# Global keys behind 96 own keys of each block, and one normalising step for a block on VectorE

## The chip, the core and the metric

The kernel runs on one core of one Trainium2 chip. The metric is the device time of one execution in microseconds (us); less is better. The engines of the core are named as in the profile: PE is TensorE (PEld its weight loads), DVE is VectorE, ACT is ScalarE, POOL is GpSimd, SP is SyncE, whose queue issues the DMAs.

## The reference: local and global attention, then a gated FFN

There are 8 batches of 8 heads, 512 local and 32 global tokens, heads of 64 dimensions, all in float32. Global tokens attend to all 544 keys. A local token attends to the 32 global keys and to local keys at most 32 positions away. The heads of a batch are then joined to rows of 512, and every row goes through a gated feed-forward network (FFN) with 1536 hidden units.

```python
k_all = np.concatenate([k_g, k_l], axis=2)
out_g = np.matmul(sm(scale * np.matmul(q_g, k_all.transpose(0, 1, 3, 2))), v_all)
mask = np.abs(pos[:, None] - pos[None, :]) <= 32
s_ll = np.where(mask, scale * np.matmul(q_l, k_l.transpose(0, 1, 3, 2)), -1e9)
s_lg = scale * np.matmul(q_l, k_g.transpose(0, 1, 3, 2))
out_l = np.matmul(sm(np.concatenate([s_lg, s_ll], axis=-1)), np.concatenate([v_g, v_l], axis=2))
x = concat([out_g, out_l], axis=2), heads joined: (8 * 544, 512)
out = (sigmoid(x @ w_gate) * (x @ w_val)) @ w_out
```

`sm` is a softmax with the row's maximum subtracted and 1e-9 added to the sum.

## The kernel before, in words

**Tiles of the attention.** A head's 512 local queries are four blocks of 128. The host lays the keys out so that the keys of a block stand in one window of 224 columns (`WIN`): 32 own keys left of the block, 64 of the block's first keys, the 32 global keys, the block's other 64 keys, and 32 own keys right of it. Neighbouring windows overlap and start 160 columns apart (`BLK`). Block 0 has no left and block 3 no right part, so their windows are 192 wide (`span`). `local_unit` works on two blocks at once: (0, 1) or (2, 3) where a chunk has two blocks, and (0, 3), called the joint unit, and then (1, 2), where it has four. It has four stages, between which other work is emitted:

1. scores into PSUM (L234); then VectorE adds the mask and finds the maximum (L248), and ScalarE takes the exponential with its sum (L251), both into `s_sb`, which has one buffer;
2. the reciprocal of the sums (L254, L255), and the normalised probabilities into `p_buf` (`scaled`, L214 to L219). Per block there is one instruction for the main columns (2 x 64, the block's own keys) and one for the side columns (2 or 3 pieces of 32: left, global, right). Which engine does it goes by the table `NORM`: VectorE (L218) for converted heads and the first chunk, and ScalarE (L216) or VectorE in turn for the second chunk and the first four heads of the third;
3. transposes of `p_buf` in tiles of 128 columns on PE (L271; 4, or 3 in the joint unit), copied out of PSUM by ScalarE (L282, or L279 for native heads), the remainder by VectorE (L283);
4. the products with V on PE (L302 and L303, or L294 and L295), two for each block: the main tile `VM[j]` and the side tile `VS[j]` of V, which the host filled in the same order, with zero rows where a transposed tile holds columns that aren't the block's.

**Two number formats.** From the fifth head of the third chunk on, heads are *converted*: every operand is split into a rounded part and a remainder (`split_qk` with L197 to L200, `split_v` with L210 and L211), and a product is made from the parts; there are 52 of these heads. The first 20 heads are *native* and use float32 matmuls. Of these, 12 take part in global scores within the same chunks (the eight of the second chunk and four of the third).

**Global rows.** For each head `global_scores` makes the 32 x 544 scores of the global queries in three steps: two of 256 columns (a 64-column half of all four windows, L319) and one of 32 columns (L321), each once for a native and twice for a converted head. ScalarE copies them into `pg` (L323, L324), and for four heads together `global_group` normalises, transposes five tiles (L341) and multiplies with V (L356 or L362).

**FFN and weights.** `ffn_stream` runs over chunks of up to 512 rows and 12 hidden tiles each: gate and value matmuls (L401), ScalarE's tanh, absolute value and exponential (L409 to L416) and VectorE's minimum (L414), VectorE's products (L421 to L425) with ScalarE's cast (L424), then the output matmuls (L438). The first two chunks have 256 rows and alternate. Each weight piece is loaded into one of three staging buffers and converted in `convert` by ScalarE (L137, L141), VectorE (L139, L140) and POOL (L142); the output weights go to DRAM and come back as `wo` (L429). `x_split` (L373, L374) brings the attention's result into the FFN's format.

**Order of the work.** Attention, splits, loads and conversions are events with due times in a list `queue`. `ffn_stream` yields after every few matmuls, a clock `now` advances by that amount, and all events that are due are emitted. Engines work through their own instructions in the emitted order, apart from places where `issue_after` or the scheduler moves an instruction, and wait for each other where data or buffers ask for it.

## Time and profile before

| what | value |
|---|---|
| median of 3 runs | 1164.27 us (1164.24 to 1165.34) |
| profiled execution | 1168.26 us, of which the span of the profile 1166.3 us |
| mean granted clock of PE | 0.997 |
| PE busy, of the span | 1148.5 us (98%) |
| VectorE busy | 747.2 us (64%), 2132 instructions |
| ScalarE busy | 751.9 us (64%), 1737 instructions |
| POOL busy | 413.9 us (35%) |

Busy time is the time in which at least one instruction of the engine was running by the profile. Matmuls are pipelined: a row gives the length of one from its start to its modelled end, and the distance between the starts of neighbours is what one costs in a stream. A wait is idle time of an engine in front of an instruction, with the engine or transfer that ended it. The granted clock is TensorE's, as a share of full speed.

### The profile page before, as it was taken

Reading aid. Unit: us, or ns where it says so; the run is one execution under the profiler, and the core shown is the slowest. Engines: PE = TensorE matmul, PEld = TensorE weight load, DVE = VectorE, ACT = ScalarE, POOL = GpSimd, SP = SyncE. Lnnn points to the kernel's source line nnn. Section 1 sums busy time; section 2 is a strip of 40 time slices with the busy share of each in tenths; the row PEclk is TensorE's granted clock in tenths of the full one; section 3 lists DMA queues with packets and bytes.
Section 4 is the critical chain, followed back from the end, with each engine's and each line's share of the span. In section 5 each row is a group of like instructions: output and inputs, shape, how many; then the busy total and the mean of one; then the engine's idle time right before and its main releaser. Section 6 shows DMA issues by size and latency. Waiting matters only on the chain.

```text
span 1166.3 us, 19141 instructions
## 1 busy us (share of the span) xinstructions
PE 1148.5 (98%) x6596; PEld 962.8 (83%) x6596; DVE 747.2 (64%) x2132; ACT 751.9 (64%) x1737; POOL 413.9 (35%) x408
## 2 busy tenths in 40 slices
PE   8999999999999999999999999999999999999998
PEld 6777788988888888888888888888888888888897
DVE  5667746666776677667676677667676677533343
ACT  5898867666676766667675676676675676432343
POOL 2434434424443444434443444334452443100000
PEclk9999999999999999999999999999999999999999
DMA  8888844334333333343443343343344342122143
GB/s 295 285 278 272 270 126 117 117 114 113 111 101 129 117 107 109 107 130 100 117 117 104 116 117 99 108 136 101 109 118 126 97 125 74 56 89 72 55 157 115
DMA packets 59489, 151.81 MB, mean 130 GB/s; under 512 B 6144, under 2 KB 19456, under 8 KB 59392
## 3 DMA queue, kind: packets, MB, share of 16 engines
q1 hardware_dynamic: 59392, 150.59, 42.4%
q8 instruction: 52, 0.85, 0.3%
q14 instruction: 45, 0.37, 0.1%
HBM read 135.36 MB, written 15.20 MB: 129 GB/s over the span
## 4 chain that ended last, share of the span: by engine, by line
PE 90%; ACT 3%; DMA 2%; DVE 2%; POOL 1%; issue 1%; SPq 0%; DVEq 0%; ACTq 0%; POOLq 0%
PE bank_g L401 23%; PE bank_o L438 23%; PE bank_v L401 23%; PE bank_x L234 5%; PE bank_y L271 4%; PE bank_x L319 2%; PE bank_x L302 2%; PE bank_x L303 2%; PE bank_x L362 1%; PE bank_o L110 1%; PE bank_x L294 1%; DMA wo<-wo_dram 1%; PE bank_y L341 1%; PE bank_x L295 1%; DMA xt<-in_w_val_dram 1%
## 5 line engine op out<-in xcount | busy, mean ns | idle before, releaser
L438 PE MATMUL bank_o<-wo,hh 128*128 128x512 f32 x1224 | 330.4, 401 | 3.3 <-ACT hh L424 1.7
L401 PE MATMUL bank_g<-xt,wg 128*128 128x512 f32 (+1 forms) x1440 | 330.8, 365 | 0.1
L401 PE MATMUL bank_v<-xt,wv 128*128 128x512 f32 (+1 forms) x1440 | 328.4, 364 | 0.0
L401 PEld LDWEIGHTS bank_g<-xt,wg 128*128 128x128 f32 x1440 | 237.1, 189 | 37.6 <-issue 2.7
L401 PEld LDWEIGHTS bank_v<-xt,wv 128*128 128x128 f32 x1440 | 237.2, 189 | 36.0 <-DVE t L306 1.5
L438 PEld LDWEIGHTS bank_o<-wo,hh 128*128 128x128 f32 x1224 | 218.0, 189 | 44.1 <-ACT hh L424 3.5
L251 ACT ACTIVATE s_sb<-s_sb,nm 128x192 f32<-128x192 f32 (+1 forms) x240 | 110.5, 462 | 96.0 <-DVE nm L248 95.6
L211 POOL TENSOR_TENSOR vhl<-v_raw,vhl 128x512 fp32r<-128x512 f32 x52 | 67.4, 1296 | 185.5 <-ACT vhl L210 102.7
L307 POOL TENSOR_TENSOR x<-t 64x256 f32<-64x256 f32 x104 | 76.6, 736 | 156.9 <-DVE t L306 130.9
L218 DVE TENSOR_SCALAR p_buf<-s_sb,r 128x128 f32<-128x128 f32 (+2 forms) x443 | 124.8, 312 | 6.3 <-PE bank_y L271 1.8
L198 POOL TENSOR_TENSOR kl<-qk_raw,qk_hi 128x704 fp32r<-128x704 f32 x52 | 88.7, 1705 | 111.8 <-ACT qk_hi L197 111.3
L424 ACT CAST hh<-bank_v 128x512 fp32r<-128x512 f32 (+1 forms) x120 | 62.7, 522 | 91.3 <-DVE bank_v L422 90.3
L409 ACT ACTIVATE th<-bank_g 128x512 f32<-128x512 f32 (+1 forms) x120 | 63.9, 532 | 86.6 <-PE bank_g L401 86.2
L414 DVE TENSOR_SCALAR mn<-bank_g 128x512 f32<-128x512 f32 (+1 forms) x108 | 67.5, 625 | 72.5 <-ACT th L409 72.5
L306 DVE TENSOR_TENSOR t<-bank_x,t 64x512 f32<-64x512 f32 x104 | 70.7, 680 | 66.8 <-ACT t L305 66.2
L248 DVE CUSTOM_DVE_ANT_0 s_sb<-bank_x,masks 128x192 f32<-128x192 f32 (+1 forms) x240 | 79.9, 370 | 38.7 <-PE bank_x L234 34.4
L421 DVE TENSOR_TENSOR bank_v<-bank_v,mn 128x512 f32<-128x512 f32 (+1 forms) x120 | 73.8, 615 | 48.1 <-PE bank_v L401 43.7
L425 DVE TENSOR_TENSOR hh<-bank_v,hh 128x512 fp32r<-128x512 f32 (+1 forms) x120 | 72.9, 608 | 32.6 <-ACT hh L424 30.6
L200 POOL TENSOR_TENSOR qk_hi<-qk_raw,qk_hi 64x256 fp32r<-64x256 f32 x104 | 80.2, 792 | 4.1
L283 DVE TENSOR_TENSOR pt<-bank_y,pt 128x384 fp32r<-128x384 f32 x104 | 64.2, 618 | 21.5 <-ACT pt L282 21.3
L422 DVE SCALAR_TENSOR_TENSOR bank_v<-th,bank_v 128x512 f32<-128x512 f32 (+1 forms) x120 | 73.3, 611 | 1.7
L271 PE MATMUL bank_y<-ident,p_buf 128*128 128x128 f32 x440 | 70.0, 275 | 1.9 <-DVE mn L414 0.9
(108 smaller groups left out, 1654.0 us busy)
## 6 DMA issues: line engine op xcount, KB each, us to landing
wo<-wo_dram SPq DMA_DIRECT2D x116, 512.0 KB, 3.4
qk_raw<-in_qk_dram SPq DMA_DIRECT2D x104, 312.0 KB, 4.5
v_raw<-in_v_dram SPq DMA_DIRECT2D x52, 256.0 KB, 2.6
out_dram<-ob SPq DMA_DIRECT2D x34, 256.0 KB, 2.9
xt<-in_w_gate_dram SPq DMA_DIRECT2D x12, 512.0 KB, 5.1
xt<-in_w_val_dram SPq DMA_DIRECT2D x12, 512.0 KB, 4.8
xt<-in_w_out_dram SPq DMA_DIRECT2D x12, 512.0 KB, 5.6
v_nat<-in_v_dram SPq DMA_DIRECT2D x8, 512.0 KB, 8.0
```

The costliest lines, as they stand in the source:

```text
L198: nc.gpsimd.tensor_tensor(kl, t[:, K0:Q1], hi[:, K0:Q1].bitcast(F32), op=ALU.subtract)
L200: nc.gpsimd.tensor_tensor(hi[64:128, r], t[64:128, r], hi[64:128, r].bitcast(F32), op=ALU.subtract)
L218: nc.vector.tensor_scalar(out, in_, by, None, op0=ALU.mult)
L248: anchor[0] = nc.vector.tensor_tensor_reduce(out=s_sb[:, i, w], in0=s_ps[:, i, w], in1=mid[:, w], scale=-0.125, scalar=3.0e38, op0=ALU.add ...
L251: exp_at[0] = nc.scalar.activation(s_sb[:, i, w], s_sb[:, i, w], AF.Exp, bias=nm[:, i:i + 1], scale=-1.0, accum_out=sm[:, i:i + 1])
L271: nc.tensor.transpose(pt_ps[:, t], flat[:, t * P:(t + 1) * P], ident)
L307: nc.gpsimd.tensor_tensor(dst, t0[:, :, 0], t0[:, :, 1], op=ALU.add)
L401: nc.tensor.matmul(acc, w[a][:, t, fs], xt[:, c, t, x0:x0 + ntok], start=n == 0, stop=n == 11)
L421: nc.vector.tensor_tensor(acc, acc, mn, op=ALU.mult)
L422: nc.vector.scalar_tensor_tensor(acc, th, 1.0, acc, op0=ALU.add, op1=ALU.mult)
L425: nc.vector.tensor_tensor(hh[:, 1, 0:ntok], acc, hh[:, 0, 0:ntok].bitcast(F32), op=ALU.subtract)
L438: nc.tensor.matmul(o_ps[t], ph[:, a, t * P:(t + 1) * P], pwo[:, c], start=f2 == 0 and i == 0, stop=f2 == NF - 1 and i == 2)
```

## The change

In a window the global keys move behind the block's first 96 own keys: a window is now 32 keys left of the block, 96 of the block, the 32 global keys, the block's last 32, and 32 right of it (block 0 still has no left and block 3 no right part). So the columns of a block go into `p_buf` in the order in which they stand in `s_sb`, and one VectorE instruction normalises all 192 or 224 of them. `NORM` and `scaled` are gone, and with them ScalarE's share. Two blocks stand behind each other in `p_buf` at the offsets of a table `PLACE`, which also says where the 128-column tiles for the transposes start; `KEYS` names the two tiles of V of each block. V's eight tiles are filled in the new order, again with zero rows. A transposed tile may now hold columns of the neighbouring block, which meet zero rows of V. The global scores are taken in steps of 192 columns (all of block 3's window), 256 (128 each of blocks 1 and 2) and 96 (block 0), and stand in `pg` from column 64 on.

```diff
-VM = (0, 1, 4, 5)
-VS = (2, 3, 6, 7)
+T0, J0, X1, Y1, X2, Y2, J3, T3 = range(8)
+NV = 8
+V_GLOBAL = (J3, T3, X1, X2, T0)
+KEYS = {0: (T0, J0), 1: (X1, Y1), 2: (X2, Y2), 3: (J3, T3)}
+PLACE = {(0, 1): ((-32, 192), ((T0, 0), (J0, 128), (X1, 192), (Y1, 320))),
+         (2, 3): ((0, 224), ((X2, 0), (Y2, 128), (J3, 160), (T3, 288))),
+         (1, 2): ((0, 224), ((X1, 0), (Y1, 128), (X2, 224), (Y2, 352))),
+         (0, 3): ((-32, 192), ((T0, 0), (J0, 128), (T3, 256)))}
+G0 = 64
-NORM = {0: "v", 1: "v", 2: "ssv", 3: "sv"}
...
-    for c0, lo, hi in ((0, 0, 64), (128, 96, -32)):
-        cols = mid[:, c0:c0 + 96]
+    for c0, nc0, lo, hi in ((0, 128, 0, 64), (160, 64, 128, -64)):
+        cols = mid[:, c0:c0 + nc0]
...
-    p_bufs = [const.tile([P, 2, 256], F32, name="p_buf"),
-              ffn.tile([P, 512], F32, name="p_first", tag="mn", bufs=1).rearrange("p (a c) -> p a c", a=2)]
+    p_bufs = [const.tile([P, 480], F32, name="p_buf"),
+              ffn.tile([P, 512], F32, name="p_first", tag="mn", bufs=1)]
     nc.vector.memset(p_bufs[0], 0.0)
-    nc.vector.memset(p_bufs[1][:, :, WIN - SG:], 0.0)
+    nc.vector.memset(p_bufs[1][:, 416:448], 0.0)
...
-    def scaled(kind, out, in_, by):
-        if NORM[kind][cnt["norm"] % len(NORM[kind])] == "s":
-            nc.scalar.mul(out, in_, by)
-        else:
-            nc.vector.tensor_scalar(out, in_, by, None, op0=ALU.mult)
-        cnt["norm"] += 1
...
-        flat = pb.rearrange("p a c -> p (a c)")
-        joint = blocks[0] == 0 and blocks[1] == 3
+        places, tiles = PLACE[tuple(blocks)]
         for i, j in enumerate(blocks):
-            main = s_sb[:, i, 32:224].rearrange("p (a c) -> p a c", c=96)[:, :, 0:64]
-            m0, s0 = 256 * i, (0 if joint else 256 * i) + P + (64 if j == 3 else 0)
+            w0, w1 = span(j)
             with tc.issue_after(low_at[0].ins) if not nat and blocks[0] == 1 else nullcontext():
-                scaled(nat, flat[:, m0:m0 + P].rearrange("p (a c) -> p a c", c=64), main, r[:, i:i + 1])
-            n = 2 if j in (0, 3) else 3
-            side = s_sb[:, i].rearrange("p (a c) -> p a c", c=32)[:, 3 * (j == 0):7:3][:, 0:n]
-            scaled(nat, flat[:, s0:s0 + 32 * n].rearrange("p (a c) -> p a c", c=32), side, r[:, i:i + 1])
+                nc.vector.tensor_scalar(pb[:, places[i] + w0:places[i] + w1], s_sb[:, i, w0:w1], r[:, i:i + 1], None,
+                                        op0=ALU.mult)
...
-        for t in range(nt):
-            nc.tensor.transpose(pt_ps[:, t], flat[:, t * P:(t + 1) * P], ident)
+        for t, (_, c) in enumerate(tiles):
+            nc.tensor.transpose(pt_ps[:, t], pb[:, c:c + P], ident)
...
-            nc.tensor.matmul(o_ps[:, i], vt[:, VM[j], :], pt[:, :, 2 * i, :], start=True, stop=False)
-            nc.tensor.matmul(o_ps[:, i], vt[:, VS[j], :], pt[:, :, side_at[i], :], start=False, stop=True)
+            for n, tl in enumerate(KEYS[j]):
+                nc.tensor.matmul(o_ps[:, i], vt[:, tl, :], pt[:, :, at[tl], :], start=n == 0, stop=n == 1)
...
-        for half in range(2):
-            o0 = 96 * half
-            for t, (src, k0) in enumerate(zip(ks, k0s)):
-                view = src[:, k0 + 32:k0 + 32 + 4 * BLK].rearrange("p (j c) -> p j c", c=BLK)[:, :, o0:o0 + 64]
-                nc.tensor.matmul(sa[:, :, 64 * half:64 * half + 64], qg, view, start=t == 0, stop=t == last)
         for t, (src, k0) in enumerate(zip(ks, k0s)):
-            nc.tensor.matmul(sb, qg, src[:, k0 + 96:k0 + 128], start=t == 0, stop=t == last)
+            nc.tensor.matmul(sa[:, 0:192], qg, src[:, k0 + 3 * BLK:k0 + 3 * BLK + 192], start=t == 0, stop=t == last)
+        for t, (src, k0) in enumerate(zip(ks, k0s)):
+            view = src[:, k0 + BLK:k0 + 3 * BLK].rearrange("p (j c) -> p j c", c=BLK)[:, :, 0:P]
+            nc.tensor.matmul(sa[:, 192:448].rearrange("p (j c) -> p j c", c=P), qg, view, start=t == 0, stop=t == last)
+        for t, (src, k0) in enumerate(zip(ks, k0s)):
+            nc.tensor.matmul(sb, qg, src[:, k0 + 32:k0 + 128], start=t == 0, stop=t == last)
-        nc.scalar.copy(pg[rows, 0:SL], sa.rearrange("p a c -> p (a c)"))
-        nc.scalar.copy(pg[rows, SL:KALL], sb)
+        nc.scalar.copy(pg[rows, G0:G0 + 448], sa)
+        nc.scalar.copy(pg[rows, G0 + 448:G0 + KALL], sb)
...
-        scaled(0, p, p, mg[:, 3:4])
+        nc.vector.tensor_scalar(p, p, mg[:, 3:4], None, op0=ALU.mult)
...
-        ke[:, o:o + 64] = kl[:, j * P:j * P + 64]
-        ke[:, o + 64:o + 96] = kg
-        ke[:, o + 96:o + 160] = kl[:, j * P + 64:(j + 1) * P]
+        ke[:, o:o + 96] = kl[:, j * P:j * P + 96]
+        ke[:, o + 96:o + 128] = kg
+        ke[:, o + 128:o + 160] = kl[:, j * P + 96:(j + 1) * P]
```

More of the change, by code (lines that the diff above doesn't have):

```diff
@@ L100 @@
     wo_dram = [dram.tile([P, 2, DM], F32, name=f"wo_dram{f}") for f in range(NF)]
-    cnt = {"p": 0, "norm": 1}
+    cnt = {"p": 0}
     fill_ps = ps.tile([P, DM], F32, name="bank_o3")
@@ L186, in load_v @@
             return
-        t = raw.tile([P, 8, D], F32, name="v_raw")
+        t = raw.tile([P, NV, D], F32, name="v_raw")
         nc.sync.dma_start(t[:, c], v[n][:, c])
@@ L207, in split_v @@
         t = T["v_raw"]
-        vhl = spl.tile([P, 8, 2 * D], F32R, name="vhl", bufs=GH + 1)
+        vhl = spl.tile([P, NV, 2 * D], F32R, name="vhl", bufs=GH + 1)
         with tc.issue_after(exp_at[0].ins):
@@ L293, in local_unit @@
             for i, j in enumerate(blocks):
-                nc.tensor.matmul(o_ps[:, i], vt[:, VM[j], :], pt[:, 2 * i], start=True, stop=False)
-                nc.tensor.matmul(o_ps[:, i], vt[:, VS[j], :], pt[:, side_at[i]], start=False, stop=True)
+                for n, tl in enumerate(KEYS[j]):
+                    nc.tensor.matmul(o_ps[:, i], vt[:, tl, :], pt[:, at[tl]], start=n == 0, stop=n == 1)
             if T["first"]:
@@ L301, in local_unit @@
         for i, j in enumerate(blocks):
-            nc.tensor.matmul(o_ps[:, i], vt[:, VM[j], :], pt[:, :, 2 * i, :], start=True, stop=False)
-            nc.tensor.matmul(o_ps[:, i], vt[:, VS[j], :], pt[:, :, side_at[i], :], start=False, stop=True)
+            for n, tl in enumerate(KEYS[j]):
+                nc.tensor.matmul(o_ps[:, i], vt[:, tl, :], pt[:, :, at[tl], :], start=n == 0, stop=n == 1)
         t0 = att.tile([64, 2, 2, P], F32, name="t0", tag="t0", bufs=1)
@@ L355, in global_group @@
                 for j in range(5):
-                    nc.tensor.matmul(o_ps[:, r], pt[:, j, r, 0], T["v"][:, tiles[j], :], start=j == 0, stop=j == 4)
+                    nc.tensor.matmul(o_ps[:, r], pt[:, j, r, 0], T["v"][:, V_GLOBAL[j], :], start=j == 0,
+                                     stop=j == 4)
             nc.scalar.copy(xg, o_ps)
@@ L361, in global_group @@
             for j in range(5):
-                nc.tensor.matmul(o_ps[:, r], pt[:, j, r].rearrange("p c q -> p (c q)"), T["v"][:, tiles[j], :],
+                nc.tensor.matmul(o_ps[:, r], pt[:, j, r].rearrange("p c q -> p (c q)"), T["v"][:, V_GLOBAL[j], :],
                                  start=j == 0, stop=j == 4)
@@ L574, in host_layout @@
     vg = v_g.reshape(N, SG, D)
-    ve = np.zeros((N, 8, P, D), np.float32)
     for j in range(4):
         o = 32 + j * BLK
-        ke[:, o:o + 64] = kl[:, j * P:j * P + 64]
-        ke[:, o + 64:o + 96] = kg
-        ke[:, o + 96:o + 160] = kl[:, j * P + 64:(j + 1) * P]
-        ve[:, VM[j]] = vl[:, j * P:(j + 1) * P]
-        s = 64 if j == 3 else 0
-        if j > 0:
-            ve[:, VS[j], s:s + 32] = vl[:, j * P - 32:j * P]
-            s += 32
-        ve[:, VS[j], s:s + 32] = vg
-        if j < 3:
-            ve[:, VS[j], s + 32:s + 64] = vl[:, (j + 1) * P:(j + 1) * P + 32]
+        ke[:, o:o + 96] = kl[:, j * P:j * P + 96]
+        ke[:, o + 96:o + 128] = kg
+        ke[:, o + 128:o + 160] = kl[:, j * P + 96:(j + 1) * P]
+    ve = np.zeros((N, NV, P, D), np.float32)
+    for tl, row, parts in ((T0, 0, (vl[:, 0:96], vg)), (J0, 0, (vl[:, 96:160],)),
+                           (X1, 0, (vl[:, 96:224],)), (Y1, 0, (vg, vl[:, 224:288])),
+                           (X2, 0, (vl[:, 224:352],)), (Y2, 0, (vg, vl[:, 352:416])),
+                           (J3, 64, (vl[:, 352:416],)), (T3, 0, (vl[:, 416:480], vg, vl[:, 480:512]))):
+        rows = np.concatenate(parts, axis=1)
+        ve[:, tl, row:row + rows.shape[1]] = rows
     ql = q_l.reshape(N, SL, D)
```

21 lines of the change are left out of this document (11 added, 10 removed).

## The prediction

> **What bounds the kernel now.** I read the page first, then the stretches of the span, then what TensorE waited for, then single groups and instructions. The page:
>
> ```profile
> span 1166.3 us, 19141 instructions
> PE 1148.5 (98%) x6596; PEld 962.8 (83%) x6596; DVE 747.2 (64%) x2132; ACT 751.9 (64%) x1737; POOL 413.9 (35%) x408
> ```
>
> TensorE (PE) is without work for 1166.3 - 1148.5 = 17.8 us only. VectorE (DVE) and ScalarE (ACT), the engines that the change relieves, are busy 64%. Where the 17.8 us lie is seen by stretches (columns: window, then busy time and count of PE, PEld, DVE, ACT, POOL, granted clock, DMA share, GB/s):
>
> ```profile
> 30.00:60.00 30.00, 27.75 (x179) 21.20 (x179) 21.08 (x64) 26.77 (x75) 12.04 (x11) 1.00 0.82 277
> 90.00:120.00 30.00, 28.23 (x206) 22.94 (x206) 24.35 (x63) 26.70 (x73) 12.97 (x10) 1.00 0.84 274
> 300.00:600.00 300.00, 299.55 (x1662) 250.95 (x1662) 206.13 (x595) 201.77 (x444) 129.37 (x127) 1.00 0.38 111
> ```
>
> From 300 to 600 us PE lacks 0.45 us of 300: there nothing that VectorE saves can show. In the ramp (to about 150 us, where the weights are loaded and converted beside the first attention heads) PE lacks 2.25 us of 30, ScalarE is at 26.77/30 = 89% and the DMA engines at 82%. PE's own waits, whole run (total, times, longest):
>
> ```profile
> PE bank_x L234 <- DMA qk_nat<-in_qk_dram: 3.8, 1, 3.8
> PE bank_x L302 <- DVE pt L283: 1.7, 5, 0.5
> PE bank_o L438 <- ACT hh L424: 1.7, 3, 0.9
> PE bank_x L294 <- ACT pt_nat L279: 1.6, 2, 1.0
> PE bank_o L438 <- DMA wo<-wo_dram: 1.5, 1, 1.5
> PE bank_y L271 <- DVE mn L414: 0.9, 1, 0.9
> PE bank_x L294 <- ACT pt_first L279: 0.7, 1, 0.7
> PE bank_y L321 <- DVE mn L414: 0.6, 1, 0.6
> PE bank_y L271 <- ACT mn L411: 0.5, 1, 0.5
> PE bank_y L271 <- ACT p_buf L216: 0.4, 1, 0.4
> ```
>
> The first is the first load and stays. L302 on DVE is the only one behind the ramp: 1.7 us. The rest, 1.7+1.6+1.5+0.9+0.7+0.6+0.5+0.4 = 7.9 us, is the ramp's.
>
> **The change part by part.**
>
> *Normalising on VectorE.* It was four instructions a unit of two blocks (main and side columns of each), and is two. The rows of the old ones (line, shape, count, busy, mean ns):
>
> ```profile
> L218 DVE TENSOR_SCALAR p_buf<-s_sb,r 128x128 f32<-128x128 f32 x230 | 67.7, 314 | 1.9
> L218 DVE TENSOR_SCALAR p_buf<-s_sb,r 128x64 f32<-128x64 f32 x107 | 33.3, 312 | 0.0
> L218 DVE TENSOR_SCALAR p_buf<-s_sb,r 128x96 f32<-128x96 f32 x106 | 31.4, 308 | 4.4 <-PE bank_y L271 1.8
> ...
> L216 ACT ACTIVATE p_buf<-s_sb,r 128x96 f32<-128x96 f32 x14 | 4.8, 370 | 1.8 <-DVE r L255 1.7
> L216 ACT ACTIVATE p_buf<-s_sb,r 128x64 f32<-128x64 f32 x13 | 4.0, 341 | 0.3 <-DVE r L255 0.3
> L216 ACT ACTIVATE p_buf<-s_sb,r 128x128 f32<-128x128 f32 x10 | 3.8, 398 | 0.0
> ...
> L218 DVE TENSOR_SCALAR p_first<-s_first,r 128x128 f32<-128x128 f32 x8 | 2.3, 284 | 0.1
> ...
> L218 DVE TENSOR_SCALAR p_first<-s_first,r 128x64 f32<-128x64 f32 x4 | 1.0, 248 | 0.0
> ```
>
> In the p_first rows 64 columns more cost 284 - 248 = 36 ns, so one instruction of 192 contiguous columns should take 320 ns and one of 224 some 338 (estimate), with the 30 ns by which the p_buf row stands above (314 against 284) 350 and 370. It is bounded by 320 ns below and by the two that it replaces, 314+312 = 626 ns, above; I take 360, near the lower end, because width costs so little in these rows. VectorE loses 67.7+33.3+31.4 = 132.4 us and in the first chunk 32 instructions of some 0.28 = 9 us, and gains 128 units x 2 x 0.36 = 92: about 49 us less of 747.2. On PE's path this is worth nothing from 300 us on: PE's matmuls cover it, and if they did not, a unit would gain some 0.5 us.
>
> *ScalarE's share.* The three L216 rows, 37 instructions and 4.8+4.0+3.8 = 12.6 us, leave ScalarE, all of them in the ramp's second chunk and the first half of the third. These 16 units (8 in the second chunk, 8 of the third's first four heads) had 64 instructions, so VectorE had 27 of them: 27 x 0.31 = 8.4 us, and will have 32 x 0.36 = 11.5. ScalarE, the fullest engine there, loses 12.6 us, VectorE gains 3 on 21 to 24 of 30 us. Queued behind these on VectorE are the conversion of the weights (L139, L140), the minimum (L414) and the products L421 to L425, each of which PE meets a few matmuls later; behind those on ScalarE are th and mn (L409 to L416), hh and the casts. I take 1.0 us of the 7.9 as gained: one wait names p_buf on ScalarE, others stand one or two instructions behind it, but much of the ramp goes by the loads (0.82 to 0.84 busy), and an earlier PE meets them earlier. Bounds: all 7.9 gained; or 4 us lost, if VectorE's extra 3 us fall on waits and 1 us more is lost around them.
>
> *The steady wait.* In the chain of work that ended last, ahead of the longest run of such waits:
>
> ```profile
> 186.31 1.10 DVE p_buf L218 x4
> ...
> 191.58 0.36 PE bank_x L302
> ```
>
> Four normalisations of 1.10 us become two of about 0.65, so what follows comes 0.45 us earlier, nearly the longest of the five waits (0.5). I take 1.0 of the 1.7 us (bounds 0 and 1.7); late next is then the cast on ScalarE or vhl on POOL, which the chain passes too.
>
> *Global scores on PE.* The matmuls stay six a converted head, three a native one, but 256+256+32 columns become 192+256+96. As PE is full, their spacing counts. Single instructions (start, duration):
>
> ```profile
> 246.41 0.28 PE L319 MATMUL bank_x<-qk_hi 128*32 128x256 f32 x1
> ...
> 246.89 0.18 PE L321 MATMUL bank_y<-qk_hi 128*32 128x32 f32 x1
> ...
> 246.95 1.17 PE L438 MATMUL bank_o<-wo,hh 128*128 128x512 f32 x4
> ...
> 251.64 0.26 PE L234 MATMUL bank_x<-qk_hi 128*128 128x192 f32 x1
> 251.73 0.27 PE L234 MATMUL bank_x<-kl,qk_hi 128*128 128x192 f32 x1
> 251.84 0.27 PE L234 MATMUL bank_x<-qk_hi 128*128 128x192 f32 x1
> ...
> 619.24 1.36 PE L362 MATMUL bank_x<-vhl,ptg 128*64 128x128 f32 x20
> 620.43 0.45 PE L401 MATMUL bank_g<-xt,wg 128*128 128x512 f32 x1
> ```
>
> Four of 256 take 0.48 us from start to start (0.12 each), the two of 32 together 0.06: 0.54 a head. A 192 takes 0.09 or 0.11 (with a 128-column weight behind it, where the new one has 32: I take 0.09); a 96 lies between 0.025 (the 32) and 0.06 (128 columns: 1.19/20); I take 0.045. New: 2x0.09 + 2x0.12 + 2x0.045 = 0.51, bounds 0.47 and 0.58. Of 64 heads, 52 are converted: 52 x -0.03 = -1.6 us (-3.6 to +2.1).
>
> [...]
>
> The 12 native heads, all in the ramp:
>
> ```profile
> 39.87 1.05 PE L319 MATMUL bank_x<-qk_nat 64*32 64x256 f32 x4
> 40.76 0.22 PE L321 MATMUL bank_y<-qk_nat 64*32 64x32 f32 x2
> 40.91 0.74 PE L401 MATMUL bank_v<-xt,wv 128*128 128x256 f32 x4
> ```
>
> 0.89 + 0.15 = 1.04 us. Two of the four shrink by a quarter (0.222 each to 0.167), the last two grow from 0.075 to some 0.085: -0.09 us, 12 times -1.1 us. Half of it, -0.5, I count, since the ramp waits for others anyway (bounds -1.1 and 0).
>
> *What costs nothing.* Transposes (4, or 3 in the joint unit) and products with V keep number and size, and both layouts give a transpose 128 contiguous columns. The two copies into pg take 448 and 96 columns instead of 512 and 32, the same sum, with nobody behind them but the next reduction. Masks and memsets lie under the first load's 3.8 us. DMAs keep number and size, so SP's queue passes the same things.
>
> **Sum.** -1.6 - 0.5 - 1.0 - 1.0 = -4.1 us. The profiled execution took 1168.26 us (span 1166.3 and 2 us around it), 4.0 above the median 1164.27; it would become 1164.2, and the median 1160.2. A change under 0.2% (2.3 us) can't be told from none here.
>
> **The rivals.**
>
> *Nothing arrives (30%).* PE's spacing is set by weight loads and not by columns, and the ramp goes by its loads. For it: DMA share 0.82 to 0.84; 192 columns at 0.11 in one of two rows. Against it: 32 and 128 columns do go faster than 256. With bursts at 0.54 and the ramp unmoved only part of the steady waits is left: 1163.7.
>
> *A stall goes, and a slow clock with it (13%).* The worst stretch of the ramp:
>
> ```profile
> 145.00:150.00 5.00, 5.00 (x20) 3.82 (x18) 0.00 (x0) 0.62 (x3) 0.93 (x1) 0.51 0.43 146
> ...
> 133.55 1.67 PE L438 MATMUL bank_o<-wo,hh 128*128 128x512 f32 x6
> ...
> 143.89 2.93 PE L438 MATMUL bank_o<-wo,hh 128*128 128x512 f32 x6 [1.49 <-DMA wo<-wo_dram]
> ```
>
> After waits of 0.6 (mn), 0.6 (pt_nat) and 1.5 (wo) in a row PE runs at clock 0.51 for 5 us: 2.45 us lost, seen in six matmuls at 2.93 instead of 1.67. If ScalarE's relief takes the first two waits away, 1.2 + 2.45 go beyond the sum: 1156.5. Against it: the third wait is a load.
>
> [...]
>
> *VectorE becomes the late engine of the ramp: slower (12%).* Its 3 us more fall on the in-order conversions; once waits as near together as those at 141 to 144 us come up a second time, a second half clock follows: 2.7 us idle and 2.45 of clock, against the 2.1 that PE's bursts save and with the steady gain lost, 1167.3. It decides from about 4.4 us of new waits on. Against it: VectorE has 6 to 9 us of 30 free.
>
> **How the numbers follow.** Forecast 45%, rivals 30, 13 and 12. The likeliest, 1160.2, has a range of its own from 1157 to 1164, by the bounds of the bursts and half of those of the ramp. The range, 1155.5 to 1166, takes in the second rival whole and leaves out the slower one and the ramp's far ends. Faster: 0.40 of the forecast's 0.45 and the 0.13, 0.53. Same: 0.05 of the forecast and nearly all of the first rival, 0.34. Slower: 0.13.
>
> **What would show it.** Right: PE's busy and matmul counts unchanged, L218 in groups of 192 and 224 at 320 to 380 ns, x256 in all, no L216 instructions; a head's global scores in 0.51 us; L302's wait under 1 us. Wrong: VectorE's L218 near 600 ns; 96-column matmuls spaced at 0.11; a clock under 0.9 in a second window of the ramp; new waits of PE on DVE mn or on the converted weights.

## The result, and the profile after

The change makes the kernel slower: 1176.85 us (median of 4 runs, 1172.05 to 1179.08) against 1164.26 us before (4 runs, 1162.35 to 1165.34), ratio 1.0109 with a 95% interval of 1.0088 to 1.0129. The prediction, 1160.2 us with a range up to 1166.0, was wrong. The profiled execution of after took 1176.99 us. Its page:

```profile
span 1175.1 us, 18887 instructions
PE 1149.7 (98%) x6596; PEld 961.5 (82%) x6596; DVE 720.8 (61%) x1914; ACT 749.3 (64%) x1700; POOL 413.6 (35%) x408
```

VectorE's instructions became 44 us shorter in sum, near the 49 that were forecast (outside the first chunk its normalising went from 132.4 to 89.2 us), and ScalarE's 13 us; but the busy times fell by 26.4 and 2.6 us alone, since rows of neighbours overlap (in a row of after shown below, t runs from 411.01 to 411.69 us and pt starts at 411.61) and busy time counts an overlap once. PE is without work for 25.4 us instead of 17.8. Stretches of after, the first and the last of which the prediction showed of before (window, then busy time and count of PE, PEld, DVE, ACT, POOL, granted clock, DMA share, GB/s):

```profile
30.00:60.00 30.00, 27.04 (x148) 20.92 (x147) 19.81 (x57) 23.48 (x60) 12.69 (x11) 0.83 0.73 245
...
170.00:300.00 130.00, 125.92 (x820) 109.32 (x820) 81.23 (x235) 88.23 (x213) 52.34 (x52) 1.00 0.39 114
300.00:600.00 300.00, 296.96 (x1645) 247.40 (x1644) 191.97 (x518) 202.38 (x443) 126.36 (x125) 1.00 0.38 111
```

From 300 to 600 us PE now lacks 3.04 us, where it lacked 0.45. That is the surprise: the loss stands in the part that the prediction had called full. Two things make up the 12.6 us: the steady part and the ramp.

**The steady part.** The FFN matmuls come in the same order in both traces but for one output matmul a batch, so one can compare the start of the matmul of the same number. Between the one at 152 us of before and the one at 1032 us, after falls back by 10.9 us (from 2.1 ahead to 8.8 behind). I use this *lag* below for every kernel; before's own is zero. Of after's 10.9 us, 2.7 arise up to 228 us and 8.2 behind it. PE's waits in after, whole run (total, times, longest):

```profile
PE bank_x L300 <- DVE pt L280: 4.2, 12, 1.0
...
PE bank_v L398 <- DVE t L303: 2.6, 6, 0.4
PE bank_x L292 <- ACT pt_nat L276: 2.5, 2, 2.1
PE bank_y L318 <- DVE mn L411: 1.4, 2, 1.0
PE bank_x L300 <- DVE mn L411: 1.3, 7, 0.2
```

L300, L280, L398 and L303 of after are before's L302, L283, L401 and L306. The wait for pt was 1.7 us in 5 pieces and is 4.2 in 12; the waits for t are new, and those for the minimum are new behind the ramp.

**The ramp.** The slow stretch at 145 us is gone, as my second rival had it, and another has come at 30 to 50 us, where the products with V waited 2.1 us for pt_nat (before ran these 20 us at a clock of 1.00):

```profile
30.00:40.00 10.00, 7.24 (x34) 5.59 (x33) 6.21 (x16) 7.20 (x17) 4.46 (x4) 0.68 0.75 249
40.00:50.00 10.00, 10.00 (x58) 8.34 (x58) 6.71 (x23) 7.22 (x22) 3.77 (x3) 0.81 0.75 255
...
145.00:150.00 5.00, 5.00 (x35) 4.24 (x35) 1.42 (x4) 3.66 (x10) 1.36 (x2) 1.00 0.81 252
```

By the mean clock it isn't in every run: of after's four, one had a mean clock of 1.000 and a span of 1170.2 us, three had 0.994 to 0.996 and 1174.7 to 1177.1. So by my estimate some 5 us of these three runs hang on it (10 x 0.32 + 10 x 0.19 = 5.1 us by the two slow rows above, 4.5 to 6.9 us by the spans), and 9 to 11 us of each on the steady part. The two add up to more than 12.6 us, since before lost some time to the clock too (2.45 us at 145 us in its profiled execution). The experiments are about the steady part.

### The profile page after: what moved, and what is told of

Its sections match the earlier page's. It is cut to its first block, busy times and chain, and to the rows that moved or that the text cites. A ratio compares the mean times of both kernels' runs of the same rounds, so it can differ in the third digit from the quotient of the medians.

```text
span 1175.1 us, 18887 instructions
## 1 busy us (share of the span) xinstructions
PE 1149.7 (98%) x6596; PEld 961.5 (82%) x6596; DVE 720.8 (61%) x1914; ACT 749.3 (64%) x1700; POOL 413.6 (35%) x408
## 4 chain that ended last, share of the span: by engine, by line
PE 71%; DVE 12%; ACT 12%; issue 3%; DMA 1%; POOL 1%; DVEq 0%; ACTq 0%; SPq 0%
PE bank_g L398 19%; PE bank_v L398 18%; PE bank_o L435 18%; PE bank_x L234 4%; PE bank_y L268 3%; PE bank_x L300 3%; ACT s_sb L251 3%; DVE p_buf L260 2%; DVE pt L280 1%; PE bank_x L292 1%; DVE bank_v L419 1%; PE bank_x L359 1%; DVE bank_v L418 1%; ACT mn L412 1%; DVE t L303 1%
## 5 line engine op out<-in xcount | busy, mean ns | idle before, releaser
L398 PE MATMUL bank_v<-xt,wv 128*128 128x512 f32 (+1 forms) x1440 | 328.8, 364 | 2.6 <-DVE t L303 2.6
L398 PE MATMUL bank_g<-xt,wg 128*128 128x512 f32 (+1 forms) x1440 | 330.7, 365 | 0.2 <-DVE t L303 0.2
L435 PE MATMUL bank_o<-wo,hh 128*128 128x512 f32 x1224 | 326.0, 398 | 0.8 <-ACT hh L421 0.7
L398 PEld LDWEIGHTS bank_v<-xt,wv 128*128 128x128 f32 x1440 | 237.5, 189 | 40.0 <-DVE t L303 4.0
L398 PEld LDWEIGHTS bank_g<-xt,wg 128*128 128x128 f32 x1440 | 237.9, 190 | 37.4 <-issue 2.5
L303 DVE TENSOR_TENSOR t<-bank_x,t 64x512 f32<-64x512 f32 x104 | 70.8, 681 | 86.4 <-ACT t L302 85.3
L248 DVE CUSTOM_DVE_ANT_0 s_sb<-bank_x,masks 128x192 f32<-128x192 f32 (+1 forms) x240 | 80.9, 370 | 35.9 <-PE bank_x L234 31.3
L418 DVE TENSOR_TENSOR bank_v<-bank_v,mn 128x512 f32<-128x512 f32 (+1 forms) x120 | 73.7, 614 | 43.9 <-PE bank_v L398 38.5
L260 DVE TENSOR_SCALAR p_buf<-s_sb,r 128x192 f32<-128x192 f32 (+1 forms) x240 | 88.6, 397 | 2.1
L280 DVE TENSOR_TENSOR pt<-bank_y,pt 128x384 fp32r<-128x384 f32 x104 | 64.4, 619 | 36.3 <-ACT pt L279 36.3
L300 PEld LDWEIGHTS bank_x<-pt,vhl 128*128 128x128 f32 x416 | 61.0, 188 | 23.5 <-issue 7.8
```

The source lines that it names most:

```text
L248: anchor[0] = nc.vector.tensor_tensor_reduce(out=s_sb[:, i, w], in0=s_ps[:, i, w], in1=mid[:, w], scale=-0.125, scalar=3.0e38, op0=ALU.add ...
L260: nc.vector.tensor_scalar(pb[:, places[i] + w0:places[i] + w1], s_sb[:, i, w0:w1], r[:, i:i + 1], None, op0=ALU.mult)
L300: nc.tensor.matmul(o_ps[:, i], vt[:, tl, :], pt[:, :, at[tl], :], start=n == 0, stop=n == 1)
L303: nc.vector.tensor_tensor(t0, o_ps[0:64], t0, op=ALU.add)
L398: nc.tensor.matmul(acc, w[a][:, t, fs], xt[:, c, t, x0:x0 + ntok], start=n == 0, stop=n == 11)
L418: nc.vector.tensor_tensor(acc, acc, mn, op=ALU.mult)
```

## Where the steady part loses: three engines' rows, before and after

The program emits work in one order, and a scheduler lays down each engine's queue from it before the run. I compared these queues. Around 407 us, where the products of a unit of blocks (0,3) are finished and those of (1,2) begin, ScalarE's rows of before read (start, duration):

```profile
407.04 0.17 ACT L324 COPY pg_buf<-bank_y 32x32 f32<-32x32 f32 x1
407.24 0.58 ACT L305 COPY t<-bank_x 64x512 f32<-64x512 f32 x1
407.73 1.23 ACT L197 CAST qk_hi<-qk_raw 128x1248 fp32r<-128x1248 f32 x1
408.98 0.59 ACT L282 CAST pt<-bank_y 128x512 fp32r<-128x512 f32 x1
```

and of after:

```profile
408.81 0.23 ACT L321 COPY pg_buf<-bank_y 32x96 f32<-32x96 f32 x1
409.06 1.24 ACT L204 CAST qk_hi<-qk_raw 128x1248 fp32r<-128x1248 f32 x1
410.32 0.58 ACT L302 COPY t<-bank_x 64x512 f32<-64x512 f32 x1
410.93 0.59 ACT L279 CAST pt<-bank_y 128x512 fp32r<-128x512 f32 x1
```

The 1.23 us cast of the next head's q and k has gone ahead of t, the copy of the finished products. VectorE in before:

```profile
407.93 0.68 DVE L306 TENSOR_TENSOR t<-bank_x,t 64x512 f32<-64x512 f32 x1 [1.88 <-ACT t L305]
409.05 0.70 DVE L421 TENSOR_TENSOR bank_v<-bank_v,mn 128x512 f32<-128x512 f32 x1 [0.44 <-PE bank_v L401]
409.66 0.68 DVE L283 TENSOR_TENSOR pt<-bank_y,pt 128x512 fp32r<-128x512 f32 x1
...
410.85 0.35 DVE L248 CUSTOM_DVE_ANT_0 s_sb<-bank_x,masks 128x192 f32<-128x192 f32 x1
...
411.12 0.35 DVE L248 CUSTOM_DVE_ANT_0 s_sb<-bank_x,masks 128x192 f32<-128x192 f32 x1
...
411.59 0.69 DVE L425 TENSOR_TENSOR hh<-bank_v,hh 128x512 fp32r<-128x512 f32 x1
```

and in after:

```profile
411.01 0.68 DVE L303 TENSOR_TENSOR t<-bank_x,t 64x512 f32<-64x512 f32 x1 [3.24 <-ACT t L302]
411.61 0.67 DVE L280 TENSOR_TENSOR pt<-bank_y,pt 128x512 fp32r<-128x512 f32 x1
412.21 0.68 DVE L418 TENSOR_TENSOR bank_v<-bank_v,mn 128x512 f32<-128x512 f32 x1
...
413.53 0.35 DVE L248 CUSTOM_DVE_ANT_0 s_sb<-bank_x,masks 128x192 f32<-128x192 f32 x1
...
414.28 0.69 DVE L422 TENSOR_TENSOR hh<-bank_v,hh 128x512 fp32r<-128x512 f32 x1 [0.39 <-ACT hh L421]
414.89 0.35 DVE L248 CUSTOM_DVE_ANT_0 s_sb<-bank_x,masks 128x192 f32<-128x192 f32 x1
```

VectorE sits idle 3.24 us for t instead of 1.88. Then pt stands ahead of the first product (L418) instead of behind it, and hh stands between the two maxima (L248). All that follows starts later, until PE's product of the next unit waits for pt. These three swaps, the cast on ScalarE, pt and hh on VectorE, stand in 12 places each, two a batch from the third batch on. They are not all: GpSimd's x changes its place in as many, and ScalarE's th and hh in 12 and 6 more. TensorE's order in the steady part is the same but for one output matmul a batch, which before makes some 5 us earlier (427.31 against 432.30 us in one case). That isn't the cause: old_score_steps_again below has it in after's place and loses nothing, and new_steps_old_layout has it in before's and loses more.

## The experiments

Ratios are to the kernel before, run on the same chip (its medians there were 1162.97 to 1163.74 us); all compare with after's 1.0109.

### Is it the place behind pt?

My first theory was that the whole step, now behind `issue_after(low_at)`, is late, where before only the main columns were. before_anchored puts before's side columns there too:

```diff
-            scaled(nat, flat[:, s0:s0 + 32 * n]...
+            with tc.issue_after(low_at[0].ins) if not nat and blocks[0] == 1 else nullcontext():
+                scaled(nat, flat[:, s0:s0 + 32 * n]...
```

> The kernel before with one edit: in the units (1, 2) of converted heads the side instructions too are queued behind the remainder pt (L283), as the whole normalising step is after the change. Theory A (the place in VectorE's queue: with the whole step behind pt, VectorE idles ahead of pt and then has more in a row ahead of mn and t): most of the steady loss of about 11 us appears here, 1170 to 1175 us, with PE idle of 2 to 3 us between 300 and 600 us. Theory B (the scheduler parts the two maxima of a unit by hh, which waits): VectorE's order here has no such parted pair, so 1163 to 1166. Theory C (longer instructions meet POOL more often): 1163 to 1166.

1167.81 us, ratio 1.0047 (1.0027 to 1.0068): in the old layout the place costs 4 us, in which five t that the scheduler moved on ScalarE and VectorE have an unknown share. The other way round, after with the step free of the edge, wholly (no_anchor), for the second block of a unit (second_block_anchored; despite its name, the edge stays on the first block's instruction: `... and i == 0`), or for the second of two pieces of each block, cut at column 128 (four_pieces):

> The changed kernel without that queueing at all: both instructions of a unit (1, 2) go ahead of pt in most units. Theory A: VectorE's idle time ahead of pt is filled, 1163 to 1169 us, unless pt now comes too late for the products with V (then the wait of L300 on pt grows and it stays above 1170). Theories B and C: 1173 to 1178.

> The changed kernel with only the first block's instruction of the units (1, 2) queued behind pt; the other may go ahead of it. One 224-column instruction stands ahead of pt and one behind. Theory A: about half or more of the steady loss goes, 1165 to 1170 us. Theories B and C: no change, 1173 to 1178.

> The changed kernel with each block's step cut in two contiguous pieces, columns up to 128 (queued behind pt in the units (1, 2), as the main part was before) and the rest (free). VectorE has the same number of normalising instructions as before and two of them ahead of pt again; the pairs of maxima are still parted by hh in its order. Theory A: the steady loss goes, 1163 to 1168 us, the rest being the ramp's. Theory B: it stays, 1172 to 1178. Theory C: it goes, 1163 to 1168.

no_anchor 1182.52 us, 1.0154 (1.0127 to 1.0182); second_block_anchored 1173.34, 1.0076 (1.0051 to 1.0101); four_pieces 1182.78, 1.0160 (1.0129 to 1.0190). Freed, the steps go ahead of pt and hold it up. no_anchor on VectorE, and then on PE:

```profile
405.01 1.61 DVE L260 TENSOR_SCALAR p_buf<-s_sb,r 128x224 f32<-128x224 f32 x2
406.55 0.55 DVE L280 TENSOR_TENSOR pt<-bank_y,pt 128x384 fp32r<-128x384 f32 x1
```

```profile
407.24 1.17 PE L398 MATMUL bank_v<-xt,wv 128*128 128x512 f32 x4 [0.85 <-DVE pt L280]
```

Here two steps of 224 columns take 1.61 us ahead of pt, and PE's bank_v, whose buffer pt has to empty, waits 0.85 us: 12 such waits, 10.2 us. So nothing says that the place behind pt made after slow: leaving it wholly costs more, and with one of two steps (1.0076) it can't be told from after. The cut into more, shorter instructions (four_pieces) doesn't help either. A third guess, that instructions of VectorE meet GpSimd's, is not settled by that; it is taken up with old_steps_four_pieces below.

### Is it the global scores' step sizes?

old_score_steps is after with steps of 256, 256 and 32 columns, two halves of 64 columns of all four windows and 32 columns more (they cover other key columns than they should), and nothing else changed:

```diff
-        sa = ps.tile([SG, 448], F32, name="bank_x", tag="att", bufs=4)
-        sb = ps.tile([SG, 96], F32, name="bank_y", tag="att", bufs=4)
...
+        sa = ps.tile([SG, 4, P], F32, name="bank_x", tag="att", bufs=4)
+        sb = ps.tile([SG, SG], F32, name="bank_y", tag="att", bufs=4)
```

> The changed kernel, but a head's global scores are taken in steps of 256, 256 and 32 columns again, from the new layout as it lies (so the global rows are made of other key columns; work and sizes are those of before). The scheduler's order on VectorE then has no parted maxima. Theory B (the order that the scheduler makes with the new step sizes costs most): the steady loss falls from 10.9 us to about 5, what is left being the place behind pt; 1168 to 1172 us, although PE's bursts go back to 0.54 us a head. Theory A alone (the place behind pt is all of it): 1174 to 1179.

> Both undone in the new layout: global scores in steps of 256, 256 and 32 columns (of other key columns, as in the run before this), and each block's normalising step in two pieces, the second of them free to go ahead of pt. If theories A and B together are the whole cause, it is like the kernel before: 1162 to 1167 us, under 1.5 us of PE waits from 170 us on. If something else in the new layout costs (which columns a transpose reads, the order of the tiles), it stays above 1170.

> The same kernel as old_score_steps, for a trace that can be read. Order theory: 1162 to 1164.5; behind 170 us TensorE's idle time is within 2 us of before's (1.7 us), VectorE's waits for hh between the two maxima are gone, and the low part of pt stands behind the first product. If the whole step behind pt cost by itself there would be waits for pt of 2 us or more, as in before_anchored.

old_score_steps took 1163.0 us, 0.9995 (0.9976 to 1.0014), and again 1164.28, 1.0003 (0.9991 to 1.0016): all of the loss is gone, with the whole step behind pt and two instructions a unit. One of the ten executions of the first took 3428.99 us, and the ratio leaves it out. With the step cut and its second pieces free (old_steps_four_pieces) it is 1178.83, 1.0114 (1.0075 to 1.0154). In the units (1, 2) its normalising instructions have before's number, places and column counts, and behind 228 us all else on the four engines comes in before's order, so the place alone can't explain it. What differs is their form. before's free ones take three pieces of 32 columns, the new ones one piece of 96. VectorE and GpSimd in before, and then in old_steps_four_pieces:

```profile
403.73 0.53 DVE L218 TENSOR_SCALAR p_buf<-s_sb,r 128x96 f32<-128x96 f32 x2
403.88 1.29 POOL L211 TENSOR_TENSOR vhl<-v_raw,vhl 128x512 fp32r<-128x512 f32 x1 [2.03 <-ACT vhl L210]
```

```profile
405.67 1.48 DVE L262 TENSOR_SCALAR p_buf<-s_sb,r 128x96 f32<-128x96 f32 x2
405.75 1.33 POOL L218 TENSOR_TENSOR vhl<-v_raw,vhl 128x512 fp32r<-128x512 f32 x1 [2.03 <-ACT vhl L217]
```

In the second trace the later of the two pieces ends just behind GpSimd's instruction. So it is in all 12 places where PE's bank_v waits for pt there (9.6 us in all): this piece takes 1294 to 1298 ns, where a piece that meets no GpSimd instruction has a median of 265. In before, 50 instructions of three pieces began while GpSimd ran one, and none took more than 314 ns. So in these 12 places a normalising instruction that is in one piece and meets GpSimd ahead of pt costs PE time; no_anchor and four_pieces, whose instructions take one piece each as well, have 12 waits of bank_v for pt each (10.2 and 9.9 us in all). That prices these versions and not after, whose step stands behind pt as in old_score_steps. Then the mirror, the kernel before with steps of 192, 256 and 96:

```diff
+        for t, (src, k0) in enumerate(zip(ks, k0s)):
+            view = src[:, k0 + 32 + BLK:k0 + 32 + 4 * BLK].rearrange("p (j c) -> p j c", c=BLK)[:, :, 0:64]
+            nc.tensor.matmul(sa[:, 0:192].rearrange("p (j c) -> p j c", c=64), qg, view, start=t == 0, stop=t == last)
...
+            nc.tensor.matmul(sb, qg, src[:, k0 + 32:k0 + 128], start=t == 0, stop=t == last)
```

> The kernel before, old key layout and four normalisations a unit, but with the global scores in steps of 192, 256 and 96 columns, as the change has them (of other key columns: which key lands in which column of the scores is left to differ). VectorE's static order then parts the two maxima of one unit in 11 of the (0,3) units a steady pattern has (hh between them) and puts pt ahead of the first product, as after. Order theory: that order alone costs, so slower than before: 1170 to 1175, with TensorE waiting 8 us or more behind 170 us for pt, t and bank_v's minimum, of which before has 1.7. Layout theory (the long normalisation behind pt is what costs, and the order only where that stands): 1161.5 to 1164.5, since 52 bursts of 0.03 us are saved and nothing is lost.

1179.75 us, 1.0151 (1.0127 to 1.0175). Its waits behind 170 us are after's:

```profile
PE bank_x L302 <- DVE pt L283: 4.4, 12, 1.0
PE bank_v L402 <- DVE t L306: 2.0, 6, 0.3
...
PE bank_x L302 <- DVE mn L415: 0.6, 4, 0.2
```

So the step sizes alone make the loss, in either layout and with either way of normalising. The expectation of 1170 to 1175 was too low, in part, by my estimate, since its runs had more of the ramp's slow clock (a mean of 0.993 to 0.997; in the profiled one 0.77 from 30 to 60 us and 0.93 from 145 to 170 us); its lag, 12.4 us, is above after's as well.

### Is it VectorE's order?

order_restored raises the priority of the two maxima, so that they stand together again; order_and_one_ahead frees the second block's step as well; order_whole holds pt of the units of blocks (1,2) behind the first product:

```diff
+            with tc.high_priority(offset=20):
+                anchor[0] = nc.vector.tensor_tensor_reduce(
...
+                with tc.issue_after(after.ins) if after is not None else nullcontext():
+                    low_at[0] = nc.vector.tensor_tensor(pt[:, 1], pt_ps, pt[:, 0].bitcast(F32), op=ALU.subtract)
```

> The changed kernel with its own step sizes 192, 256 and 96, and the two maxima of a unit emitted to the scheduler with a higher priority, so that hh no longer stands between them and t comes behind the first normalising instruction, as before; nothing else is touched and the step still stands whole behind pt. Theory B by the order itself: most of B's share goes, steady loss 4 to 7 us, 1167 to 1173. If the sizes themselves cost and not the order: no change, 1174 to 1179.

> order_restored, and the second block's instruction free to go ahead of pt. If A and B add up, the steady loss is 0 to 3 us, 1162 to 1167; it would be the first version with the new layout that is no slower than before. If the free instruction only makes pt late, it is no better than the run before this.

> The change with the maxima of a unit raised in priority and the low part of pt of the units of blocks (1,2) held behind the first product (L418) where that is emitted in between: VectorE's steady order is then that of old_score_steps, maxima, first product and pt, with the score steps of 192, 256 and 96 columns. Order theory: the 5 us that order_restored still lacked were the place of pt, so 1160 to 1164 (old_score_steps took 1163.0, and the bursts save 52 x 0.03 = 1.6 us on top). Size theory: the 96-column step itself, its PSUM tile or its copy costs the 5 us, so 1167 to 1169, with the waits for pt at some 2.7 us as in order_restored.

1168.2 us, 1.0037 (1.0020 to 1.0054); 1169.09, 1.0040 (1.0020 to 1.0060); 1168.23, 1.0040 (1.0028 to 1.0053). By these times two thirds of the loss come back with the maxima, and pt's place adds nothing. By the lag it is half (5.3 us are left in order_restored), since none of its ten runs had the ramp's slow clock of after (their means are 0.998 to 1.000, and the profiled one had 1.00 from 30 to 60 us, where after had 0.83). order_whole still loses 4.8 us of lag against old_score_steps_again's 0.4. The size theory of order_whole's expectation had the right number here; how far it was right is seen from the last run.

### Is it ScalarE's order?

The cast was then held behind t with an edge. cast_behind_t sets it for every head, order_whole_cast adds it to order_whole, before_cast to the kernel before:

```diff
-        nc.scalar.copy(hi, t)
+        with tc.issue_after(t_at[-2].ins) if len(t_at) > 1 else nullcontext():
+            nc.scalar.copy(hi, t)
...
-        nc.scalar.copy(t0, o_ps[64:128])
+        t_at.append(nc.scalar.copy(t0, o_ps[64:128]))
```

> The change, with one edge more in ScalarE's order: the cast of the next head's q and k (L204, 1.23 us) is issued behind the copy t (L302) of the unit before. In the trace of after it stood ahead of t (cast 409.06, t 410.32; in before t 407.24, cast 407.73), so VectorE got t, pt and the products 1.3 us later. With this edge alone VectorE's two maxima stand together again; the low part of pt still stands ahead of the first product. ScalarE theory: the cast ahead of t is the root and all else follows from it, so 1160 to 1165 and TensorE's idle time behind 170 us within 2 us of before's. VectorE theory: its order is the cause by itself and pt ahead of the product still costs, so 1167 to 1169 as in order_restored. Size theory: the 96-column step costs the rest, 1167 to 1169 too.

> order_whole (1168.2) with the same edge on ScalarE: all orders of the steady pattern but three small swaps are then those of old_score_steps, with the new step sizes. ScalarE theory: 1160 to 1164, the 4.5 us that order_whole still lacked come back, and no wait for t or mn's reader is left. Size theory: 1167 to 1169, unchanged. If this one is faster than cast_behind_t by more than 2 us, VectorE's order costs by itself too.

> The kernel before with the same edge: there the cast already stands behind t in most units and ahead of it in some (13 and 12 places of the written order). It tells whether the edge gains by itself. ScalarE theory: before lacks only 1.7 us behind the ramp, so 1162 to 1164.5, same as before; a gain of over 2 us would say that the edge does something beyond giving back what the change lost.

All missed: 1180.83 us, 1.0147 (1.0131 to 1.0163); 1179.57, 1.0140 (1.0126 to 1.0154); 1172.77, 1.0085 (1.0071 to 1.0099). The edge was too wide. In most other units before itself has the cast ahead of t; the edge moved these as well, in 26 places more, and GpSimd's instructions with them. before_cast says only how sharply the kernel answers to this one instruction's place: 10 us. So the edge was set in the 12 places alone (`if T["h"] in (4, 7) and T["n"] >= 2 * NH`), in after and in order_whole; and before_cast_ahead turns the same 12 round in the kernel before:

```diff
+            ahead = ci >= 3 and h in (4, 7)
+            ev.append((base - sc * (15.5 if ahead else SPLIT_QK), 1, lambda T=T: split_qk(T)))
...
+        with tc.issue_after(first.pop().ins) if first else nullcontext():
+            nc.scalar.copy(t0, o_ps[64:128])
```

> The change with the edge of cast_behind_t only in the 12 places where the change had turned the order round (the casts for heads 4 and 7 of a batch, from the third batch on); in all other places the cast stays where before has it. cast_behind_t had moved it in 26 places more and so cannot tell. VectorE's maxima stand together again and GpSimd's order is before's; on VectorE the low part of pt still stands ahead of the first product (12 units). ScalarE theory: these 12 places are the root, so 1161 to 1165. Size theory, or VectorE's order on its own: 1167 to 1169, as order_restored and order_whole.

> order_whole (1168.2) with the same 12 edges: VectorE's, ScalarE's and GpSimd's order of the steady pattern as in old_score_steps but for two small swaps, with the step sizes of 192, 256 and 96. ScalarE theory: 1160 to 1164, TensorE idle 2 to 3 us behind 170 us. Size theory: 1167 to 1169, idle 7 us as in order_whole.

> The kernel before, nothing of the change in it, with the cast of q and k (1.23 us) of heads 4 and 7 written ahead of the copy t on ScalarE in those same 12 places. TensorE's order is the same in every position; on VectorE the low part of pt then stands ahead of the first product there, the maxima stay together. ScalarE theory: this is what order_whole still lacked, so 4 to 6 us slower than before, 1167 to 1170, with waits for pt, mn or t at those places. Size theory: ScalarE has room, so under 1165.

before_cast_ahead took 1172.59 us, 1.0082 (1.0056 to 1.0107), though its TensorE order is before's in every position and no score step is touched: 12 casts ahead of t, with 12 pt on VectorE and 12 x on GpSimd that moved with them, cost 9 us, more than I had expected. Its ScalarE, and its VectorE behind:

```profile
402.52 0.17 ACT L328 COPY pg_buf<-bank_y 32x32 f32<-32x32 f32 x1
402.72 1.24 ACT L198 CAST qk_hi<-qk_raw 128x1248 fp32r<-128x1248 f32 x1
403.98 0.58 ACT L309 COPY t<-bank_x 64x512 f32<-64x512 f32 x1
```

```profile
404.67 0.68 DVE L310 TENSOR_TENSOR t<-bank_x,t 64x512 f32<-64x512 f32 x1 [3.14 <-ACT t L309]
405.28 0.67 DVE L286 TENSOR_TENSOR pt<-bank_y,pt 128x512 fp32r<-128x512 f32 x1
405.88 0.68 DVE L425 TENSOR_TENSOR bank_v<-bank_v,mn 128x512 f32<-128x512 f32 x1
```

These are the same swaps of the cast and of pt as in after, with 3.14 us of waiting, in a kernel without the change; its maxima stay together. cast_two_heads took 1170.11, 1.0052 (1.0033 to 1.0071), order_whole_two_heads 1168.77, 1.0041 (1.0029 to 1.0054). With the 12 edges VectorE's maxima come together by themselves and the lag from 228 to 792 us is 0.4 us, where after's is 4.3. What is left sits mostly ahead of 228 us (2.8 us of lag) and behind 792. Ahead of it the order differs too, for three heads of the third chunk, where hh goes ahead of the 96-column copy. cast_two_heads there:

```profile
187.13 0.37 ACT L423 CAST hh<-bank_v 128x256 fp32r<-128x256 f32 x1 [0.41 <-DVE bank_v L421]
...
187.53 0.23 ACT L323 COPY pg_buf<-bank_y 32x96 f32<-32x96 f32 x1
...
190.39 0.36 PE L236 MATMUL bank_x<-qk_hi 128*128 128x192 f32 x1 [0.43 <-DVE t L305]
```

The last run therefore has the old steps for the heads before the third batch (12 native and 4 converted), the new ones for the other converted heads (48 of 52 by its trace, and not 46 as its expectation says), the 12 edges, and pt behind the product in the 12 units:

```diff
+        if T["n"] < 2 * NH:
...
+                nc.tensor.matmul(sb, qg, src[:, k0 + 160:k0 + 192], start=t == 0, stop=t == last)
```

> The change with cast_two_heads' 12 edges and with pt held behind the first product in the 12 units where it had moved ahead (blocks (1,2) of heads 2 and 5, from the third batch on), and with the old score steps of 256, 256 and 32 columns for the heads before the third batch (other key columns there), the new ones of 192, 256 and 96 behind. TensorE's order is that of old_score_steps in every position, GpSimd's too; ScalarE and VectorE differ in 12, 5 and 6 small swaps. In the trace cast_two_heads lost some 3 us against old_score_steps_again between 185 and 220 us, where hh had gone ahead of the 96-column copy for three heads. Order theory: 1162 to 1165.5, idle time from 170 to 300 us near 1 us as in old_score_steps_again, where cast_two_heads has 3.5. Size theory (96-column steps cost wherever they stand): 46 of 52 heads still have them, so 1167 to 1169.

1164.02 us, 1.0007 (0.9992 to 1.0021): the time is before's, with the new sizes in 48 of 52 converted heads and an order that is old_score_steps' but for a few small swaps. Part of this is won in the ramp, where this run too has the old steps: at 152 us it is 6.6 us ahead of before's profiled execution, cast_two_heads 5.1. The stretch from 170 to 300 us of cast_two_heads and then of this run:

```profile
170.00:300.00 130.00, 126.45 (x808) 109.91 (x805) 81.80 (x235) 88.48 (x214) 53.85 (x53) 1.00 0.39 113
```

```profile
170.00:300.00 130.00, 129.08 (x823) 112.60 (x822) 84.72 (x243) 90.21 (x217) 54.79 (x54) 1.00 0.39 115
```

PE's idle time there falls from 3.55 to 0.92 us. The lag of all these versions, by the two parts (us):

| kernel | 152 to 228 us | 228 to 1032 us |
|---|---|---|
| after | 2.7 | 8.2 |
| order_restored (maxima together, cast still ahead) | 2.7 | 2.6 |
| cast_two_heads (cast behind t) | 2.8 | 2.5 |
| order_whole_two_heads | 2.4 | 2.1 |
| new_steps_from_third_batch | -0.4 | 2.7 |
| old_score_steps_again | -0.5 | 0.9 |
| before_cast_ahead | 0.1 | 8.6 |

Behind 228 us some 5.6 of after's 8.2 us come back, with the new sizes in place, when the maxima stand together, whether by the priority or by the cast's edge. So most of this loss comes from the queues that the scheduler writes around the steps and not from their sizes. The 2.7 us ahead of 228 go only where the old steps stand there, and then the order is before's too, so size and order are not held apart in that stretch.

Four things stay open. Why the scheduler turns the order round was not tried: matmuls, PSUM tiles and copies of the steps were always changed together. The cast has no price of its own that holds in both layouts: ahead of t it costs 8.6 us of lag in before_cast_ahead, and in order_restored, with the maxima together, nothing that cast_two_heads doesn't lose as well; no run shows why, nor what GpSimd's 12 swaps do. Of the 2.7 us behind 228 that the last run still loses, against 0.9 of old_score_steps_again, the small swaps that remain or the sizes themselves can be the cause. And the ramp's slow stretch, some 5 us in three of after's four runs, was not studied by itself. No version beat the kernel before.

## Why the prediction was wrong, point by point

**Normalising on VectorE: the price a little low, the worth right.** The instructions, by form, in after:

```profile
L260 DVE TENSOR_SCALAR p_buf<-s_sb,r 128x224 f32<-128x224 f32 x120 | 44.6, 410 | 0.4
L260 DVE TENSOR_SCALAR p_buf<-s_sb,r 128x192 f32<-128x192 f32 x120 | 44.6, 385 | 1.8
```

The means are 385 and 410 ns, above the 320 to 380 that I had given; the median of both is 328 ns and the longest took 1446. The long ones are those that meet GpSimd: of all 256 in after, 54 began while GpSimd ran an instruction and took 406 to 1361 ns each, and without GpSimd beside it none took more than 336. The sum had no term for that. The relief of VectorE was put at nothing for the steady part, and old_score_steps, which has it whole, is at 0.9995 and 1.0003.

**Global scores on PE: right.** The matmuls of a head, single instructions of after, first, last and the next one:

```profile
406.12 0.25 PE L313 MATMUL bank_x<-qk_hi 128*32 128x192 f32 x1
...
406.57 0.21 PE L318 MATMUL bank_y<-kl,qk_hi 128*32 128x96 f32 x1
406.61 1.15 PE L398 MATMUL bank_v<-xt,wv 128*128 128x512 f32 x4
```

406.61 - 406.12 = 0.49 us (0.50 in another burst), where 0.51 was expected and before has 0.54. The 0.025 us that stood for a step of 32 columns is a little low: the second of before's two starts 26 to 31 ns behind the first in all 52 heads. So the spacing of the steps did fall as forecast, and the 1.6 us were lost in waits.

**"What costs nothing": the step that failed.** It said of the two copies into pg "the same sum, with nobody behind them but the next reduction". Behind them on ScalarE's queue stands the cast of q and k, and behind that t, pt and hh. I priced the new score steps as columns on PE and took the queues of the other engines as given. The scheduler wrote them anew, and where this term had nothing, after loses 10.9 us behind 152 us; with the old steps (old_score_steps_again) it is 0.4. Of the 8.2 us behind 228, 5.6 come back by order alone (order_restored). before_cast_ahead shows the other way round that order alone costs as much: 9 us without any of the change.

**"The steady wait": wrong in sign.** Four instructions of 1.10 us did become two, and yet the wait for pt grew from 1.7 to 4.2 us. In the rows above t comes late, held up on ScalarE, and pt behind it. That pt would come sooner assumed that nothing ahead of it moved.

**ScalarE's share and the ramp.** The 37 instructions are gone. The wait for pt_nat is longer (2.5 us instead of 1.6), not shorter, and the second rival's slow stretch moved from 145 to 35 us in the profiled run. That waits in a row bring the slow clock on, as the second and the third rival had it, was my reading of one stretch and was not shown: in after 2.1 and 0.7 us of waits stand beside clocks of 0.68 and 0.81, and no run changed the waits alone.

**The rivals.** The third had the right sign and the clock as one of its means, but looked for it in the ramp, at 1167.3. None had an order that changes in the steady part. The first, that nothing arrives, is what was left once the order was put back: old_score_steps has the relief of VectorE and ScalarE whole, and neither the 1.0 us of the ramp nor the 1.0 us of the wait for pt shows in its 0.9995 and 1.0003. "From 300 to 600 us nothing that VectorE saves can show" was right; it does not follow that nothing can be lost there. A PE that lacks 0.45 us of 300 shows that all others come in time, and not by how much.

## What to carry to other kernels

Where a scheduler writes the queues, a change in one place changes the order in others: before pricing a change, compare the written order of every engine, before and after, GpSimd's too, and read first what a long instruction (here a 1.23 us cast) has moved ahead of. On a bound engine without idle time, ask of each thing that it waits for how much slack it has. When an edge is meant to restore an order, set it only where the order changed: the same edge set everywhere cost 10 us in the kernel before. And before moving an instruction, look at how long it takes in its new place: in old_steps_four_pieces the normalising of 96 columns in one piece took a median of 265 ns alone and 1294 to 1298 ns in the 12 places where it met GpSimd.

## What the runs showed of the hardware

In after, PE waited 2.1 and 0.7 us in a row at 31 to 37 us, and its clock was 0.68 and 0.81 over the stretches of 10 us from 30 and from 40 us. Of one kernel, old_score_steps_again, the runs with a mean clock of 0.999 or 1.000 had spans of 1159.1 to 1162.4 us (mean 1161.0), those with 0.995 or 0.996 had 1163.4 to 1165.8 (mean 1164.5).

A VectorE instruction that normalises 192 or 224 columns in one piece took from 300 to 1446 ns in after, at most 336 ns where GpSimd ran nothing beside it and 406 to 1361 ns where GpSimd was at work at its start. Instructions on 96 columns in three pieces of 32 took 316 ns at most in before, beside GpSimd or not. In old_steps_four_pieces the same 96 columns in one piece took 1294 to 1298 ns in the 12 places beside GpSimd. What makes this difference was not shown.
